# An attention, GLU and expert kernel: the loop for surplus tokens moves ahead of the last products, and a tile's state products move up behind its output products

## Chip, cores and metric

The kernel runs on one core of a Trainium2 chip. The metric is the device time in microseconds (us) of one execution. The version before the change takes 868.49 us, the median of three runs (866.66 to 868.85).

## What is computed

Three stages follow each other on 3072 tokens (4 sequences of 768) of width 384. Cut to what matters:

```python
# 1. gated linear attention, 8 heads of 48 per token
state = alpha_t[:, None] * state + outer(k_t, v_t)      # 48 x 48 per head
y_t = q_t @ state
# 2. rms norm, then a gated unit of width 1536
xn = x / sqrt(mean(x * x) + 1e-6) * rms_g
z = (silu(xn @ w_gate) * (xn @ w_val)) @ w_out
# 3. one of 8 experts per token
e = argmax(z @ r_gate)
out = prob(e) * sigmoid(z @ r_ogate)[e] * (relu(z @ w1[e]) @ w2[e])
```

## The kernel before

**Tiles of tokens.** The attention goes over 24 tiles of 128 tokens. Tiles 0 to 17 take the first three sequences in turn (tile t is block t // 3 of sequence t % 3), tiles 18 to 23 the fourth sequence. `stages(t)` (L410) yields five functions for a tile, in this order: `score` (L420, products at L425), `ktr` (L440, transposes of k at L445, copied to `kn` by ScalarE at L447), `outp` (L452, products of the output `ps_y` at L456 and L460), `state` (L474, products `ps_st` at L481, added to the state by VectorE at L488) and `xtr` (L492, transposes at L502). The products of L460 and L481 have the same form: a weight tile of 128 x 64, 48 columns. The last block of a sequence has no `state` (L475), and the first block of one has no L456.

**The order on TensorE.** The gated unit works on 8 groups of three tiles. For each it loops over 12 blocks of the hidden width, and each block has three slots: `m_gate` (L589, nine products `ps_g`), `m_val` (L608, nine products `ps_v`) and `m_out` (L630, nine products `ps_o` of the block before). Between slots the loop asks whether a stage of the attention is due (L861, L1087); if so, `stage()` (L850) takes the next function of `att_stream` (L844), so that one stage's products go between two slots. Five stages per tile are counted (`NST`, L796). From the group loop on, `seq` (L211) keeps the products in the order of the program; in the four runs before it (L868) the framework's scheduler may still shift them.

**The experts.** Tokens are scattered to a bucket per expert. The experts, sorted by their number of tokens, get fixed capacities (`SLOTS`, L92) and are worked off in nine parts by `e_h` (L1025, products `ps_h`, then ScalarE and VectorE write `h` at L1031 and L1032) and `e_o` (L1036, products `ps_b` at L1047). `e_fin` (L1052) scales a result on ScalarE (L1059) or VectorE (L1061) and sends it out by an indirect DMA that POOL issues (L1063). The products of the last part for the last four blocks are done after the loop over the parts (L1237 to L1240):

```python
    for i in range(parts[u][3]):
        for _, j in lag:
            e_o(u, j, [i])
        e_fin(u, i)
```

**The loop for surplus tokens.** Tokens beyond a capacity are handled by a loop over `nblk` blocks of 128 (L1251), behind all of this. `nblk` is computed on the chip (`beyond`, L1141) and read into a register of each engine (L1223). The loop's body has its own products, transfers and DMA issues on all five engines. In this execution it is passed by with no iteration: no instruction of lines 1252 to 1325 stands in the trace. L1353 is the kernel's end (drains and barriers), L1342 its start.

Of the kernel before, what the change touches and what calls it, by code (L numbers as in the profile page):

```python
# [8 lines left out]
F32 = mybir.dt.float32  # L9
F32R = mybir.dt.float32r  # L10
BF16 = mybir.dt.bfloat16
I32 = mybir.dt.int32
AF = mybir.ActivationFunctionType
ALU = mybir.AluOpType
AX = mybir.AxisListType
PSUM = bass.MemoryType.PSUM
DRAM = bass.MemoryType.DRAM
OFF = bass.IndirectOffsetOnAxis
# [25 lines left out]
    'LEADG': 6,  # L44
    'NAT': 5,
    'XO': 2,
    'STRICT': 4,
    'PET': 7,
    'NO': 'arkq',
# [5 lines left out]
def gla_glu_moe_kernel(  # L55
# [16 lines left out]
    nc = tc.nc  # L72
    P = 128
    B, H, S, D = q.shape
    NT, DM = out.shape
    NP = H // 2
    NCH = S // P
    NTILE = NT // P
    KD = DM // P
# [3 lines left out]
    E, _, F2 = w1.shape  # L83
    KF2 = F2 // P
    GT = 3
# [755 lines left out]
    spread[0] = False  # L841
    prep.extend(prework(GT))

    att_stream = (st for t in range(GT, NTILE) for st in stages(t))  # L844
    nprep = GT + 1
    AHEAD = CFG['AHEAD']
    done = 0
# [293 lines left out]
    def beyond():  # L1141
# [25 lines left out]
        nc.vector.memset(obk, 0.0)  # L1167
        return tot, cb, cbx, pid, obk

    lag = []  # L1170
    pw = []

    def load_next(p):
        for i in range(4):
            pw.append((load_w1, p, i))
            pw.append((load_w2, p, i))
# [24 lines left out]
    for u in range(U):  # L1201
        for j in range(KF2):
            if u == 0 and j < 2:
                continue
            if u == U - 1 and j > 3:
                pop_o()
            e_h(u, j)
            lag.append((u, j))
            if j == 0:
                if u > 1:  # L1210
                    pop_o()
                    pop_o()
            elif j > 1 and u < U - 1:
                pop_o()
            if u and j == 0 and u + 1 < U:
                load_rows(u + 1, ers[(u + 1) % 2])
            if u and u + 1 < U and j in TRJ:
                prep_rows(u + 1, TRJ.index(j))
            for _ in range(STEPS[u][j] if u < 2 else 1):
                weight_step()  # L1220
            if u == 2 and j == 1:
                tot, cb, cbx, pid, obk = beyond()
                nblk = nc.values_load(tot[0:1, 0:1], min_val=0, max_val=NM + E)  # L1223
        if u == 0:
            pop_o()
            prep_rows(1, 0)
            prep_rows(1, 1)
            prep_rows(1, 2)
            pop_o()
        if u >= 1 and u + 1 < U:  # L1230
            while ready or pw:
                weight_step()
            if parts[u + 1][0] + 1 < E:
                addresses(parts[u + 1][0] + 1)
                load_next(parts[u + 1][0] + 1)
    u = U - 1
    for i in range(parts[u][3]):  # L1237
        for _, j in lag:
            e_o(u, j, [i])
        e_fin(u, i)  # L1240

    psE.release()
    psM.release()
    xp.release()
    wpool.release()


    with ExitStack() as ov:
        op_ = ov.enter_context(tc.tile_pool(name="op", bufs=1, side="right", reuse_waits="tile"))
        pp = ov.enter_context(tc.tile_pool(name="pp", bufs=2, space=PSUM))  # L1250
        with tc.For_i(0, nblk, 1):  # L1251
            def sm(nm, w=1, dt=F32):
                return op_.tile([P, w], dt, tag=nm, name=nm)
            V = nc.vector
            ge = sm("ge", E)
            V.tensor_scalar(out=ge, in0=cb, scalar1=obk[:, 0:1], scalar2=None, op0=ALU.is_le)
            ef = sm("ef")
            V.tensor_reduce(out=ef, in_=ge, op=ALU.add, axis=AX.X)
            oh = sm("ohx", E)
            V.tensor_scalar(out=oh, in0=io8[:, 0, :], scalar1=ef[:, 0:1], scalar2=None, op0=ALU.is_equal)  # L1260
            V.tensor_tensor(out=ge, in0=oh, in1=cnt[:, 0, :], op=ALU.mult)
            ne = sm("ne")
            V.tensor_reduce(out=ne, in_=ge, op=ALU.add, axis=AX.X)
            V.tensor_tensor(out=ge, in0=oh, in1=cbx, op=ALU.mult)
            sl = sm("sl")
            V.tensor_reduce(out=sl, in_=ge, op=ALU.add, axis=AX.X)
            V.tensor_tensor(out=sl, in0=obk, in1=sl, op=ALU.subtract)
            V.tensor_tensor(out=ge, in0=oh, in1=capE[:, :, 0], op=ALU.mult)
            ce = sm("ce")
            V.tensor_reduce(out=ce, in_=ge, op=ALU.add, axis=AX.X)  # L1270
            V.scalar_tensor_tensor(out=sl, in0=sl, scalar=float(P), in1=ce, op0=ALU.mult, op1=ALU.add)
            V.tensor_tensor(out=sl, in0=sl, in1=pid[:, 0:1], op=ALU.add)
            rw = sm("rw")
            V.scalar_tensor_tensor(out=rw, in0=ef, scalar=float(REG), in1=sl, op0=ALU.mult, op1=ALU.add)
            ri = sm("ri", 1, I32)
            V.tensor_copy(ri, rw)
            V.tensor_tensor(out=sl, in0=sl, in1=ne, op=ALU.is_lt)
            V.scalar_tensor_tensor(out=rw, in0=sl, scalar=FAR, in1=rw, op0=ALU.mult, op1=ALU.add)
            zi = sm("zi", 1, I32)
            V.tensor_copy(zi, rw)  # L1280
            nc.gpsimd.indirect_dma_start(out=bucket[:, :], out_offset=OFF(ap=zi[:, 0:1], axis=0),
                                         in_=zrow[:, 0, :], in_offset=None,
                                         bounds_check=E * REG - 1, oob_is_err=False)
            r0 = nc.values_load(ri[0:1, 0:1], engines=[mybir.EngineType.SP], min_val=0, max_val=E * REG - P)
            wi = sm("wi", KD + KF2, I32)
            wf = sm("wf", KD + KF2)
            e3 = sm("e3", 2)
            V.tensor_scalar(out=e3[:, 0:1], in0=ef, scalar1=float(DM), scalar2=None, op0=ALU.mult)
            V.tensor_scalar(out=e3[:, 1:2], in0=ef, scalar1=float(F2), scalar2=None, op0=ALU.mult)
            V.tensor_scalar(out=wf[:, 0:KD], in0=pid[:, 1:1 + KD], scalar1=e3[:, 0:1], scalar2=None, op0=ALU.add)  # L1290
            V.tensor_scalar(out=wf[:, KD:], in0=pid[:, 1 + KD:], scalar1=e3[:, 1:2], scalar2=None, op0=ALU.add)
            V.tensor_copy(wi, wf)
            xr = sm("xr", RW)
            nc.sync.dma_start(xr[:, :], bucket[bass.ds(r0, P), :])
            wa = op_.tile([P, KD, F2], F32, tag="wa", name="wa")
            wb = op_.tile([P, KF2, DM], F32, tag="wb", name="wb")
            for i in range(KD):
                nc.gpsimd.indirect_dma_start(out=wa[:, i, :], out_offset=None,
                                             in_=w1.rearrange("e k n -> (e k) n"),
                                             in_offset=OFF(ap=wi[:, i:i + 1], axis=0))  # L1300
            for i in range(KF2):
                nc.gpsimd.indirect_dma_start(out=wb[:, i, :], out_offset=None,
                                             in_=w2.rearrange("e k n -> (e k) n"),
                                             in_offset=OFF(ap=wi[:, KD + i:KD + i + 1], axis=0))
            pt = pp.tile([P, KD, P], F32, tag="pt", name="ptx")
            for i in range(KD):
                nc.tensor.transpose(pt[:, i, :], xr[:, i * P:i * P + P], ident)
            xo = op_.tile([P, KD, P], F32, tag="xo", name="xo")
            V.tensor_copy(xo, pt)
            po = pp.tile([P, DM], F32, tag="po", name="po")  # L1310
            for j in range(KF2):
                ph = pp.tile([P, P], F32, tag="ph", name="ph")
                for i in range(KD):
                    nc.tensor.matmul(ph, lhsT=wa[:, i, j * P:j * P + P], rhs=xo[:, i, :],
                                     start=(i == 0), stop=(i == KD - 1))
                ht = op_.tile([P, P], F32, tag="ht", name="ht", bufs=2)
                nc.scalar.activation(ht, ph, AF.Relu)
                nc.tensor.matmul(po, lhsT=ht, rhs=wb[:, j, :], start=(j == 0), stop=(j == KF2 - 1))
            yo = sm("yo", DM)
            V.tensor_scalar(out=yo, in0=po, scalar1=xr[:, DM:DM + 1], scalar2=None, op0=ALU.mult)  # L1320
            ti = sm("ti", 1, I32)
            V.tensor_copy(ti, xr[:, RW - 1:RW])
            nc.gpsimd.indirect_dma_start(out=out[:, :], out_offset=OFF(ap=ti[:, 0:1], axis=0),
                                         in_=yo[:, :], in_offset=None, bounds_check=NT - 1, oob_is_err=False)
            V.tensor_scalar(out=obk, in0=obk, scalar1=1.0, scalar2=None, op0=ALU.add)
    act.release()


# [29 lines left out]
```

## Time and profile before

| | |
|---|---|
| runs, us | 868.85, 868.49, 866.66 |
| profiled execution, us | 865.15 |
| its span from first to last instruction, us | 863.4 |
| TensorE (PE) busy | 840.6 us, 97% |
| VectorE (DVE), ScalarE (ACT), POOL busy | 57%, 38%, 16% |
| granted TensorE clock, mean | 0.996 of full speed |

The profiled execution's own time is 1.75 us over its span, and 3.34 us under the median of the runs. A busy share says how long an engine had something in work; products are pipelined, so the start of one product to the start of the next is the better measure of TensorE's pace. "PEld" is TensorE's loading of weights. Names like POOLq stand for an engine's sequencer, which handles waits, branches and the issue of DMAs.

### The profile page before, as it was taken

To read this page: it belongs to the slowest core of one execution; us is meant where nothing else is said; L and a number is where in the kernel's file an instruction comes from. 1 tells how busy PE (TensorE), PEld (TensorE's weight loads), DVE (VectorE), ACT (ScalarE), POOL (GpSimd) and SP (SyncE) were. 2 spreads that over 40 slices of the span, in tenths; PEclk is the share of its full clock that TensorE was granted. 3 is DMA by queue.
4 is the path that set the end of the run, shared out by engine and by line. 5 is a ranking of instruction groups with operands and counts; after the bars stand their busy time and mean duration, and the time that the engine had idled before them with its cause. 6 is when DMAs were issued, how large, how long until landed. Compare 5 with 4: busy or idle time off the path is not lost.

```text
span 863.4 us, 15649 instructions
## 1 busy us (share of the span) xinstructions
PE 840.6 (97%) x6036; PEld 806.6 (93%) x6036; DVE 491.0 (57%) x1111; ACT 324.7 (38%) x705; POOL 142.2 (16%) x204
## 2 busy tenths in 40 slices
PE   7999999999999999999999999999999999999994
PEld 5899989999999999999999999999998999999994
DVE  7998988577765655765655632343534343444320
ACT  2655543333323332333433332333235343345431
POOL 2100000001100100100010010013124242434331
PEclk9999999999999999999999999999999999999998
DMA  9964555852322222222232000041065165256510
GB/s 192 205 164 147 177 128 140 213 138 80 97 60 54 63 49 60 75 74 52 52 88 60 10 29 1 2 130 63 16 203 196 37 210 169 72 165 202 185 39 24
DMA packets 120268, 88.96 MB, mean 103 GB/s; under 512 B 55291, under 2 KB 115324, under 8 KB 120192
## 3 DMA queue, kind: packets, MB, share of 16 engines
q1 hardware_dynamic: 115728, 78.46, 34.5%
q0 software_dynamic: 4464, 9.48, 3.1%
q8 instruction: 48, 0.79, 0.4%
q14 instruction: 28, 0.23, 0.1%
HBM read 72.11 MB, written 16.07 MB: 102 GB/s over the span
## 4 chain that ended last, share of the span: by engine, by line
PE 79%; DVE 7%; issue 5%; DMA 4%; POOL 2%; SPq 1%; ACT 1%; POOLq 0%; DVEq 0%; ACTq 0%
PE ps_o L638 17%; PE ps_v L604 16%; PE ps_g L604 16%; PE ps_b L1047 9%; PE ps_h L604 9%; PE ps_s L425 3%; DMA st<-in_moe_w_dram 3%; PE ps_y L460 2%; PE ps_y L456 2%; PE ps_st L481 1%; SPq L915 1%; PE ps_k L445 1%; PE ps_x L502 1%; PE ps_t L1011 1%; POOL out_dram L1063 1%
## 5 line engine op out<-in xcount | busy, mean ns | idle before, releaser
L615 DVE TENSOR_TENSOR tt<-tt,ps_v 128x384 f32<-128x384 f32 x96 | 52.9, 551 | 119.8 <-PE ps_v L604 116.8
L618 ACT ACTIVATE hh<-tt 128x384 fp32r<-128x384 f32 x96 | 50.3, 524 | 125.2 <-DVE tt L615 119.5
L596 ACT ACTIVATE tt<-ps_g 128x384 f32<-128x384 f32 x96 | 47.1, 490 | 130.4 <-PE ps_g L604 127.3
L624 DVE TENSOR_TENSOR hl<-tt,hh 128x384 fp32r<-128x384 f32 x96 | 54.4, 566 | 27.5 <-ACT hh L618 27.3
L1032 DVE SCALAR_TENSOR_TENSOR h<-ps_h,h 128x256 fp32r<-128x256 f32 (+6 forms) x72 | 38.0, 531 | 54.2 <-ACT h L1031 53.7
L1047 PE MATMUL ps_b<-w2a,h 128*128 128x384 f32 (+2 forms) x336 | 67.4, 339 | 1.5 <-ACT h L1031 1.5
L604 PE MATMUL ps_v<-xh,wvh 128*128 128x384 f32 x192 | 66.8, 348 | 1.9 <-DVE tt L615 1.9
L604 PE MATMUL ps_g<-xh,wgh 128*128 128x384 f32 x192 | 67.9, 353 | 0.1
L638 PE MATMUL ps_o<-woh,hh 128*128 128x400 f32 x192 | 66.6, 355 | 0.4 <-ACT hh L618 0.4
L638 PE MATMUL ps_o<-wol,hh 128*128 128x400 f32 x192 | 66.4, 346 | 0.0
L1047 PE MATMUL ps_b<-w2b,h 128*114 128x384 f32 (+3 forms) x336 | 65.0, 338 | 0.2 <-ACT h L1031 0.2
L604 PE MATMUL ps_g<-xl,wgh 128*128 128x384 f32 x192 | 64.9, 338 | 0.0
L604 PE MATMUL ps_v<-xh,wvl 128*128 128x384 f32 x192 | 64.9, 338 | 0.0
L604 PE MATMUL ps_g<-xh,wgl 128*128 128x384 f32 x192 | 64.8, 338 | 0.0
L604 PE MATMUL ps_v<-xl,wvh 128*128 128x384 f32 x192 | 64.6, 336 | 0.0
L638 PE MATMUL ps_o<-woh,hl 128*128 128x400 f32 x192 | 63.5, 344 | 0.0
L1047 PEld LDWEIGHTS ps_b<-w2a,h 128*128 128x128 f32 (+2 forms) x336 | 57.5, 181 | 2.7 <-ACT h L1031 2.2
L1047 PEld LDWEIGHTS ps_b<-w2b,h 128*114 128x114 f32 (+3 forms) x336 | 57.5, 175 | 2.1 <-ACT h L1031 0.6
L604 PE MATMUL ps_h<-x,w1b 128*128 128x456 f32 (+3 forms) x288 | 58.4, 343 | 0.0
L1031 ACT ACTIVATE h<-ps_h 128x256 fp32r<-128x256 f32 (+6 forms) x72 | 33.4, 468 | 63.3 <-PE ps_h L604 63.1
L604 PE MATMUL ps_h<-x,w1a 128*128 128x256 f32 (+3 forms) x288 | 53.4, 327 | 0.0
L467 POOL TENSOR_SCALAR ss<-ss 128x1 f32<-128x1 f32 x24 | 5.9, 245 | 282.1 <-ACT xn L466 279.3
(284 smaller groups left out, 1966.0 us busy)
## 6 DMA issues: line engine op xcount, KB each, us to landing
st<-in_moe_w_dram SPq DMA_DIRECT2D x64, 384.0 KB, 4.6
bucket<-zero SPq DMA_DIRECT2D x8, 772.0 KB, 6.2
stg<-in_moe_w_gate_dram SPq DMA_DIRECT2D x12, 384.0 KB, 4.1
stg<-in_moe_w_val_dram SPq DMA_DIRECT2D x12, 384.0 KB, 4.2
stg<-in_moe_w_out_dram SPq DMA_DIRECT2D x12, 384.0 KB, 3.7
v<-in_v_dram SPq DMA_DIRECT2D x23, 192.0 KB, 3.0
blk_a<-in_alpha_dram SPq DMA_DIRECT2D x34, 96.0 KB, 2.4
blk_k<-in_k_dram SPq DMA_DIRECT2D x34, 96.0 KB, 2.2
```

The costliest lines, as they stand in the source:

```text
L425: seq(nc.tensor.matmul(ps[hh][:, p, :], lhsT=kT[r, p, :], rhs=qT[r, p, :], start=True, stop=True))
L456: seq(nc.tensor.matmul(ps[:, p * 2 * D:p * 2 * D + 2 * D], lhsT=qT[:, p, :], rhs=S_[:, p, :], start=(p == 0), stop=False, skip_group_check ...
L460: seq(nc.tensor.matmul(ps[u, h * D:h * D + D], lhsT=Pt[h % 2][:, h // 2, u], rhs=vt[t][:, h, :], start=first, stop=True, skip_group_check= ...
L596: nc.scalar.activation(tt, ps, AF.Silu)
L604: seq(nc.tensor.matmul(ps, lhsT=a_[:, kc, :], rhs=b_[:, kc, :], start=(n == 0), stop=(n == 3 * KD - 1)))
L615: nc.vector.tensor_tensor(out=tt, in0=tt, in1=ps, op=ALU.mult)
L618: nc.scalar.activation(hh, tt, AF.Copy)
L624: nc.vector.tensor_tensor(out=hl, in0=tt, in1=f(hh), op=ALU.subtract)
L638: seq(nc.tensor.matmul(obank[s][i], lhsT=a_[:, sl], rhs=weight(b_, j), start=(j == j0 and n == 0), stop=(j == j1 - 1 and n == 2)))
L1031: nc.scalar.activation(hh[:, 0, :], ps, AF.Relu)
L1032: nc.vector.scalar_tensor_tensor(out=hh[:, 1, :], in0=ps, scalar=0.0, in1=f(hh[:, 0, :]), op0=ALU.max, op1=ALU.subtract)
L1047: ins = nc.tensor.matmul(ob2[u][i][0:r], lhsT=hh[:, a_, sl], rhs=we[p][b_][:, j, :], start=(j == 0 and m == 0), stop=(j == KF2 - 1 and m = ...
```

## The change

A new generator `four(t)` stands for `stages(t)` from tile 6 on (`MT`). It still gives five functions per tile: score, transposes of k, then output products with the state products right behind them, then a function that does nothing, then the transposes of x. What the engines do with the two results after the products is called in the order output, state.

The loop for surplus tokens is now in a function `overflow()`, called behind the loop over the parts and ahead of the last 36 products and their three transfers. It stands in a condition of its own, `tc.If(nblk > 0)`. Its banks for results come from the pool of the experts, and its tiles take the place of the pool `xp`. The body is the same otherwise.

```diff
+    'MT': 6,
...
-    att_stream = (st for t in range(GT, NTILE) for st in stages(t))
+    def four(t):
+
+        s_, k_, y_, d_, x_ = stages(t)
+
+        def yd_():
+            posts = [y_(), d_()]
+
+            def post():
+                for p in posts:
+                    if p:
+                        p()
+            return post
+
+        def no_():
+            return None
+        return s_, k_, yd_, no_, x_
+
+    att_stream = (st for t in range(GT, NTILE) for st in (four if t >= CFG['MT'] else stages)(t))
...
+    def overflow():
+        xp.release()
+        op_ = tc.alloc_tile_pool(name="op", bufs=1, side="right", reuse_waits="tile")
+        with tc.If(nblk > 0):
+            with tc.For_i(0, nblk, 1):
...
+        return op_
...
+    op_ = overflow()
     u = U - 1
     for i in range(parts[u][3]):
         for _, j in lag:
             e_o(u, j, [i])
         e_fin(u, i)
 
+    op_.release()
     psE.release()
     psM.release()
-    xp.release()
     wpool.release()
-
-
-    with ExitStack() as ov:
-        op_ = ov.enter_context(tc.tile_pool(name="op", bufs=1, side="right", reuse_waits="tile"))
-        pp = ov.enter_context(tc.tile_pool(name="pp", bufs=2, space=PSUM))
-        with tc.For_i(0, nblk, 1):
...
```

## Rows read from the trace of the kernel before

**Rows 1.** Busy time by stretch: us, then busy us (instructions) of each engine, clock.

```profile
140.00:200.00 60.00, 60.00 (x491) 57.35 (x490) 39.21 (x91) 20.79 (x50) 2.61 (x8) 1.00 0.60 152
200.00:330.00 130.00, 130.00 (x1044) 124.65 (x1043) 85.05 (x204) 44.29 (x105) 14.42 (x28) 1.00 0.29 74
330.00:545.00 215.00, 215.00 (x1634) 207.45 (x1633) 117.77 (x276) 72.91 (x173) 16.43 (x33) 1.00 0.18 46
```

**Rows 2.** Timeline of PE: start, length; state products between ps_g and ps_v.

```profile
302.35 0.34 PE L604 MATMUL ps_g<-xh,wgl 128*128 128x384 f32 x1
...
302.62 0.67 PE L481 MATMUL ps_st<-v,kn 128*64 128x48 f32 x16
...
303.50 0.34 PE L604 MATMUL ps_v<-xl,wvh 128*128 128x384 f32 x1
```

**Rows 3.** Timeline of PE: output products between ps_v and ps_o.

```profile
321.12 0.34 PE L604 MATMUL ps_v<-xh,wvle 128*128 128x384 f32 x1
321.29 1.03 PE L456 MATMUL ps_y<-wide,qT 128*128 128x96 f32 x8
322.25 1.14 PE L460 MATMUL ps_y<-v,P 128*64 128x48 f32 x32
...
323.60 0.34 PE L638 MATMUL ps_o<-wol,hh 128*128 128x400 f32 x1
```

**Rows 4.** Timeline of PE at tile 6: output and state products together.

```profile
139.03 0.42 PE L604 MATMUL ps_g<-xh,wgle 128*128 128x384 f32 x1
...
141.22 0.64 PE L481 MATMUL ps_st<-v,kn 128*64 128x48 f32 x16
...
142.06 0.34 PE L604 MATMUL ps_g<-xl,wghe 128*128 128x384 f32 x1
```

**Rows 5.** Line L481 from 150 to 520 us: count, ns min/median/max.

```profile
L481 PE MATMUL ps_st<-v,kn x208: 222/222/257, 163.7 to 516.2; 128*64 128x48 f32 x104
```

**Rows 6.** Timeline of ACT: the copy of kn in the tile of rows 3.

```profile
316.72 0.60 ACT L447 ACTIVATE kn<-ps_k 128x512 f32<-128x512 f32 x1 [1.51 <-PE ps_k L445]
```

**Rows 7.** Timeline of all engines near the end.

```profile
833.15 1.64 POOL L1063 DMA_INDIRECT out_dram<-ob,ix  x1 [0.31 <-issue]
...
842.15 2.94 PE L604 MATMUL ps_h<-x,w1b 128*128 128x336 f32 x18
...
844.93 6.46 PE L1047 MATMUL ps_b<-w2b,h 128*112 128x384 f32 x36
...
845.62 0.51 DVE L1032 SCALAR_TENSOR_TENSOR h<-ps_h,h 128x336 fp32r<-128x336 f32 x1 [0.88 <-ACT h L1031]
...
852.29 0.93 POOL L1063 DMA_INDIRECT out_dram<-ob,ix  x1 [1.10 <-ACT ob L1059]
```

**Rows 8.** Line L1251, the loop's own instructions: count, ns min/median/max, first and last start.

```profile
L1251 POOLq EVENT_SEMAPHORE  x16: 17/43/2288, 853.1 to 858.0; - x16
...
L1251 PEldq EVENT_SEMAPHORE  x13: 51/51/51, 851.4 to 858.1; - x13
...
L1251 PEldq COMPARE_BRANCH  x3: 97/179/325, 848.8 to 858.2; - x3
...
L1251 POOLq INC_SWDGE_SEM  x1: 1224/1224/1224, 855.6 to 855.6; - x1
```

**Rows 9.** Line L1353, the kernel's end: the same columns.

```profile
L1353 POOLq DRAIN  x3: 40/103/4327, 858.3 to 863.2; - x3
```

**Rows 10.** Line L1342, the kernel's start: the same columns.

```profile
L1342 POOLq DRAIN  x1: 174/174/174, 0.4 to 0.4; - x1
```

**Rows 11.** Line L1223, reading nblk into registers: the same columns.

```profile
L1223 DVEq TENSOR_LOAD <-tab x1: 824/824/824, 849.4 to 849.4; - x1
```

**Rows 12.** Waits of POOL in 840 to 864 us: total, times, longest.

```profile
POOL out_dram L1063 <- ACT ob L1059: 14.4, 2, 13.3
```

**Rows 13.** Line L1063: the time from issue to landing.

```profile
DMA to landing us min/median/max: 2.7/6.1/9.4
```

**Rows 14.** The page's DMA queues: packets, MB, share of 16 engines' span.

```profile
q8 instruction: 48, 0.79, 0.4%
```

More of the change, by code (lines that the diff above doesn't have):

```diff
@@ L1168, in beyond, with sm @@
         return tot, cb, cbx, pid, obk
+    def overflow():
[3 more added lines that the diff above has]
+            with tc.For_i(0, nblk, 1):
+                def sm(nm, w=1, dt=F32):
+                    return op_.tile([P, w], dt, tag=nm, name=nm)
+                V = nc.vector
+                ge = sm("ge", E)
+                V.tensor_scalar(out=ge, in0=cb, scalar1=obk[:, 0:1], scalar2=None, op0=ALU.is_le)
+                ef = sm("ef")
+                V.tensor_reduce(out=ef, in_=ge, op=ALU.add, axis=AX.X)
+                oh = sm("ohx", E)
+                V.tensor_scalar(out=oh, in0=io8[:, 0, :], scalar1=ef[:, 0:1], scalar2=None, op0=ALU.is_equal)
+                V.tensor_tensor(out=ge, in0=oh, in1=cnt[:, 0, :], op=ALU.mult)
+                ne = sm("ne")
+                V.tensor_reduce(out=ne, in_=ge, op=ALU.add, axis=AX.X)
+                V.tensor_tensor(out=ge, in0=oh, in1=cbx, op=ALU.mult)
+                sl = sm("sl")
+                V.tensor_reduce(out=sl, in_=ge, op=ALU.add, axis=AX.X)
+                V.tensor_tensor(out=sl, in0=obk, in1=sl, op=ALU.subtract)
+                V.tensor_tensor(out=ge, in0=oh, in1=capE[:, :, 0], op=ALU.mult)
+                ce = sm("ce")
+                V.tensor_reduce(out=ce, in_=ge, op=ALU.add, axis=AX.X)
+                V.scalar_tensor_tensor(out=sl, in0=sl, scalar=float(P), in1=ce, op0=ALU.mult, op1=ALU.add)
+                V.tensor_tensor(out=sl, in0=sl, in1=pid[:, 0:1], op=ALU.add)
+                rw = sm("rw")
+                V.scalar_tensor_tensor(out=rw, in0=ef, scalar=float(REG), in1=sl, op0=ALU.mult, op1=ALU.add)
+                ri = sm("ri", 1, I32)
+                V.tensor_copy(ri, rw)
+                V.tensor_tensor(out=sl, in0=sl, in1=ne, op=ALU.is_lt)
+                V.scalar_tensor_tensor(out=rw, in0=sl, scalar=FAR, in1=rw, op0=ALU.mult, op1=ALU.add)
+                zi = sm("zi", 1, I32)
+                V.tensor_copy(zi, rw)
+                nc.gpsimd.indirect_dma_start(out=bucket[:, :], out_offset=OFF(ap=zi[:, 0:1], axis=0),
+                                             in_=zrow[:, 0, :], in_offset=None,
+                                             bounds_check=E * REG - 1, oob_is_err=False)
+                r0 = nc.values_load(ri[0:1, 0:1], engines=[mybir.EngineType.SP], min_val=0, max_val=E * REG - P)
+                wi = sm("wi", KD + KF2, I32)
+                wf = sm("wf", KD + KF2)
+                e3 = sm("e3", 2)
+                V.tensor_scalar(out=e3[:, 0:1], in0=ef, scalar1=float(DM), scalar2=None, op0=ALU.mult)
+                V.tensor_scalar(out=e3[:, 1:2], in0=ef, scalar1=float(F2), scalar2=None, op0=ALU.mult)
+                V.tensor_scalar(out=wf[:, 0:KD], in0=pid[:, 1:1 + KD], scalar1=e3[:, 0:1], scalar2=None, op0=ALU.add)
+                V.tensor_scalar(out=wf[:, KD:], in0=pid[:, 1 + KD:], scalar1=e3[:, 1:2], scalar2=None, op0=ALU.add)
+                V.tensor_copy(wi, wf)
+                xr = sm("xr", RW)
+                nc.sync.dma_start(xr[:, :], bucket[bass.ds(r0, P), :])
+                wa = op_.tile([P, KD, F2], F32, tag="wa", name="wa")
+                wb = op_.tile([P, KF2, DM], F32, tag="wb", name="wb")
+                for i in range(KD):
+                    nc.gpsimd.indirect_dma_start(out=wa[:, i, :], out_offset=None,
+                                                 in_=w1.rearrange("e k n -> (e k) n"),
+                                                 in_offset=OFF(ap=wi[:, i:i + 1], axis=0))
+                for i in range(KF2):
+                    nc.gpsimd.indirect_dma_start(out=wb[:, i, :], out_offset=None,
+                                                 in_=w2.rearrange("e k n -> (e k) n"),
+                                                 in_offset=OFF(ap=wi[:, KD + i:KD + i + 1], axis=0))
+                pt = psE.tile([P, KD, P], F32, tag="h", name="ptx", bufs=2)
+                for i in range(KD):
+                    nc.tensor.transpose(pt[:, i, :], xr[:, i * P:i * P + P], ident)
+                xo = op_.tile([P, KD, P], F32, tag="xo", name="xo")
+                V.tensor_copy(xo, pt)
+                po = psE.tile([P, DM], F32, tag="tr", name="po", bufs=1)
+                for j in range(KF2):
+                    ph = psE.tile([P, P], F32, tag="h", name="ph", bufs=2)
+                    for i in range(KD):
+                        nc.tensor.matmul(ph, lhsT=wa[:, i, j * P:j * P + P], rhs=xo[:, i, :],
+                                         start=(i == 0), stop=(i == KD - 1))
+                    ht = op_.tile([P, P], F32, tag="ht", name="ht", bufs=2)
+                    nc.scalar.activation(ht, ph, AF.Relu)
+                    nc.tensor.matmul(po, lhsT=ht, rhs=wb[:, j, :], start=(j == 0), stop=(j == KF2 - 1))
+                yo = sm("yo", DM)
+                V.tensor_scalar(out=yo, in0=po, scalar1=xr[:, DM:DM + 1], scalar2=None, op0=ALU.mult)
+                ti = sm("ti", 1, I32)
+                V.tensor_copy(ti, xr[:, RW - 1:RW])
+                nc.gpsimd.indirect_dma_start(out=out[:, :], out_offset=OFF(ap=ti[:, 0:1], axis=0),
+                                             in_=yo[:, :], in_offset=None, bounds_check=NT - 1, oob_is_err=False)
+                V.tensor_scalar(out=obk, in0=obk, scalar1=1.0, scalar2=None, op0=ALU.add)
+        return op_
@@ L1240, in gla_glu_moe_kernel @@
         e_fin(u, i)
+    op_.release()
     psE.release()
     psM.release()
-    xp.release()
     wpool.release()
-    with ExitStack() as ov:
-        op_ = ov.enter_context(tc.tile_pool(name="op", bufs=1, side="right", reuse_waits="tile"))
-        pp = ov.enter_context(tc.tile_pool(name="pp", bufs=2, space=PSUM))
-        with tc.For_i(0, nblk, 1):
[L1252 to L1325, printed above, removed]
```

## The prediction

> **What bounds the kernel now.** I read the share of each engine by stretch first. From 140 to 545 us TensorE has work in flight in all of the time, while VectorE works 39 of 60, 85 of 130 and 118 of 215 us [rows 1]: in the stretch where tiles 7 to 23 pass, the end moves with what TensorE is given, and with nothing else. Then I read the timeline of TensorE around single stages, start against start, since a busy engine may still lose time between products. Last I read the end: the last product ends at 844.93 + 6.46 = 851.39 us, and the span at 863.4, so 12.0 us have no product; a list of line L1251 and L1353 says what is in them.
>
> A difference under 0.3%, 2.6 us, can't be told from no change here.
>
> **State products behind the output products.** Inside a slot products start every 0.175 us (the 36 of ps_b: 6.46 less one length of 0.34, over 35 [rows 7]; 321.12 to 321.29 in [rows 3]). State products alone: from the last ps_g at 302.35 to the second ps_v at 303.50 are 1.15 us, where two steps would be 0.35, so the stage costs 0.80 us [rows 2]. Output products alone: 321.12 to 323.60 is 2.48, less 0.35, so 2.13 us [rows 3]. Tile 6 happens to show both together before the change: 139.03 to 142.06 is 3.03, less 0.35, so 2.68 us [rows 4]. The state products thus cost 0.55 us in company against 0.80 alone. Of the 0.55, 0.09 belong to the place, since that stage began 0.26 after the product before it and the one of rows 3 began 0.17 after. The other way of counting: 16 starts, spaced as the 32 of the same form in rows 3 (1.14 less one length of 0.22 [rows 5], over 31: 0.030 us), make 0.47. I take a saving of 0.80 - 0.48 = 0.32 us; the bounds are 0.25 and 0.33.
>
> From 150 to 520 us line L481 has 208 products, 16 per tile: 13 tiles, 7 to 14 and 18 to 22 [rows 5]; tile 6 has nothing left to win, and the others have no state products. One of the 13 shares its place with products of the routing already and I give it 0.2. The sum is 12 x 0.32 + 0.2 = 4.0 us, between 3.2 and 4.3.
>
> What could eat it: the state products read kn, which ScalarE writes from 316.72 to 317.32, in a tile whose output products begin at 321.29 [rows 6, 3]; 4 us of cover, so no wait. Without that cover each tile would lose what is missing. The result's bank is freed by the masks that the output products wait for anyway. The add of the state (L488) stands on VectorE behind ScalarE's square of the output, and it waits some 0.5 us for products already under way; behind it on VectorE stands the gated unit's product for ps_v, which is later on TensorE too. The slot that loses its stage gives VectorE and ScalarE 0.80 us less, but 21 of a group's 36 slots have no stage at all (15 stages in three tiles), and rows 1 show no wait there. No DMA is moved by this part: the load of v stays in the fifth stage. SP's and POOL's queues keep their order.
>
> **The loop leaves the end.** Behind the last DMA issue, which lasts from 852.29 to 853.22 [rows 7], POOL waits 2.29 us for the landing, until 855.4, spends 1.22 on INC_SWDGE_SEM from 855.6, then works off some 12 waits until its drain begins at 858.3 [rows 8, 9]. That drain takes 4.33 us, and the end comes 0.8 behind it. With the loop gone from here, POOL is free for its drain at 853.2, 1.8 us behind the last product, beside the landing. The trace has no drain under these circumstances. Nearest in place is the one of 4.33; the shortest, at the start of the kernel, takes 0.17 [rows 10]. With 4.33 the end comes 1.8 + 4.33 + 0.8 = 6.95 us behind the last product instead of 12.0, 5.05 less. With 0.17 the landing sets the end: 4.0 + 0.2 + 0.8 = 5.0, so 7.0 less. If the drain begins only behind the landing, 4.0 + 4.33 + 0.8 = 9.15, so 2.85 less. I take 5.05, because the 4.33 stands in the same place and nothing in the new place holds POOL back; the ends of the range are 2.85 and 7.0, and zero if the drain waits for something that I don't see.
>
> **The loop enters the middle.** It now stands between the last ps_h, which end at 842.15 + 2.94 = 845.09, and the first of the 36 ps_b, which started at 844.93 [rows 7]. TensorE has to read nblk, branch, wait for its own last product, branch again. Reading and first branch cost nothing: the sequencer did its first branch at 848.8 with products running until 851.39 [rows 8, 7], and this lead of 2.6 us covers them. The rest is exposed: 0.16 of overlap lost, 0.05 for the wait, 0.33 for the longest branch, some 0.2 for a weight load, and 0.15 of gaps. I estimate 0.9 us. It can't be under 0.3 (overlap, wait and the shortest branch of 0.10); above, it is 3.7 if all engines wait for each other as they do now behind the loop. That is worked out so: VectorE's last piece of h ends at 846.13 [rows 7], its read of nblk takes 0.82 [rows 11], two branches 0.1, the 12 waits 1.4 (from 856.9 to 858.3) and TensorE's branch 0.33, so 848.8.
>
> POOL's share is hidden. Its last issue ends at 834.8 [rows 7] and it then waits 13.3 us for ScalarE [rows 12]. The landing takes 9.4 at most [rows 13], from 833.15 to 842.6; 1.22 and even a drain of 4.33 behind that end at 848.1, where the next issue came before and now comes 0.9 later. With less cover, the three transfers at the end would begin later by what is missing. SP has nothing left to do. The reads of nblk by ScalarE and VectorE move ahead of the last three results, which aren't due before 847 (12 products behind 844.93). The indirect DMAs of the loop don't run.
>
> **The sum**, against the profiled execution's own 865.15 us: -4.0 - 5.05 + 0.9 = -8.15, so 857.0. The median is 3.34 above this execution, and I forecast the same difference there: 868.49 - 8.15 = 860.3 us.
>
> **Rivals.** *The drain is short.* Its 4.33 may be the tail of INC_SWDGE_SEM, the one thing that POOL did behind its issues; at the kernel's start, with no transfer yet, both are short. Then 858.4. *The drain follows the landing*: 862.5. *The jump costs a code fetch.* Code comes in by a queue of its own, 48 packets in 0.4% of 16 engines' span, 1.15 us each [rows 14]; today no stretch of TensorE's work contains a jump, so the trace neither shows nor excludes a stall. If the code behind the loop's body has to be fetched first, add 1.2 to 2: 861.9.
> The Trainium skill, Runtime: NRT & Kernel Launch, section Instruction fetch mechanics, says that a taken branch whose target lies outside the two blocks held by an engine forces such a fetch before it goes on. By that rule this rival holds if the body reaches over the window; no row here shows it.
> *The state products gain nothing*, because what follows a stage waits or is shifted by the scheduler where order is not kept (tiles 7 and 8); against it speak tile 6 and rows 1: 864.3. *The engines meet at the condition, without a drain*: 3.7 instead of 0.9, 863.1. *Slower than before:* the condition is a full meeting of the engines with POOL's drain inside: 848.5 when all have arrived and waited (as above), 4.33 of drain, 0.8 to the release: 853.6, a hole of 8.5 us in TensorE, while the end keeps a drain behind the landing. -4.0 + 8.5 - 2.85 = +1.65: 870.1. This decides from a hole of 6.85 us on. For it: today's skipped loop does end in such a meeting. Against it: the meeting belongs to the loop's exit, and the condition passes by the loop with its exit.
>
> **Chances and range.** Forecast 0.33 (its own range 858.8 to 861.6); short drain 0.24; drain behind the landing 0.12; code fetch 0.11; state products without gain 0.06; meeting without drain 0.05; slower 0.05; 0.04 for another order by the scheduler, of either sign. The range 856.5 to 865.0 runs from the short drain with the upper bound of the first part and a run's scatter (868.85 to 866.66) to the state products without gain. Faster by over 0.3% (under 865.9): 0.87; the slower rival at its price and the edges of two others are within 0.3%: 0.10; slower 0.03.
>
> **What would show it.** Line L481 without a group of its own from 150 us on; output and state products together near 2.6 us; TensorE still without a wait there. A pause of TensorE of some 0.7 us between the last ps_h and the first ps_b at L1047, and INC_SWDGE_SEM well ahead of the last issues. From the last product to the end 7 us, with the length and the start of POOL's last drain. A hole over 3 us at the condition, or 10 us and more behind the last product, would make the forecast wrong.

## The result, and the profile after

The changed kernel takes 857.19 us, the median of four runs (855.82 to 857.58), beside 867.58 us for the kernel before (865.88 to 868.85). The ratio is 0.9872, with a 95% interval of 0.9845 to 0.99. The profiled execution takes 857.01 us with a span of 855.2 us at a mean granted clock of 0.998. A second timing on another chip gave 858.14 beside 867.99 us, 0.9881 (0.9851 to 0.9912). The forecast was 860.3 us, a ratio of 0.9906: inside the second interval, just over the edge of the first, and 3.1 us above the time, which lies outside the forecast's own range of 858.8 to 861.6 and inside the whole one. The profiled execution fell by 8.14 us, from 865.15 to 857.01, where the sum forecast 8.15. That agreement is partly luck, as a division of the span shows. The borders are starts of single products in the timeline of TensorE (products of ps_g are counted from 0).

| stretch, us | before | after | difference | forecast |
|---|---|---|---|---|
| start to ps_g no. 108 | 120.56 | 120.26 | -0.30 | 0 |
| ps_g no. 108 to no. 720: 13 joined tiles | 410.30 | 406.04 | -4.26 | -4.0 |
| on to the first ps_h | 80.57 | 80.40 | -0.17 | 0 |
| first ps_h to last ps_h: experts | 233.35 | 234.53 | +1.18 | 0 |
| last ps_h to the end of the last product | 6.61 | 6.98 | +0.37 | +0.9 |
| last product to the end of the span | 12.04 | 6.99 | -5.05 | -5.05 |

The second stretch begins and ends with these two products before the change:

```profile
120.56 0.42 PE L604 MATMUL ps_g<-xh,wgh 128*128 128x384 f32 x1
...
530.86 0.34 PE L604 MATMUL ps_g<-xh,wghe 128*128 128x384 f32 x1
```

and with these after it:

```profile
120.26 0.42 PE L605 MATMUL ps_g<-xh,wgh 128*128 128x384 f32 x1
...
526.30 0.34 PE L605 MATMUL ps_g<-xh,wghe 128*128 128x384 f32 x1
```

The three touched stretches give 8.94 us. The expert stage gave 1.2 back, and it is the stretch that scatters: in the eleven other profiles below it takes 232.9 to 235.3 us, 235.27 in a second profile of the kernel before itself.

**The joined tile.** TensorE's timeline after the change, at the tile of [rows 3]: start, length, engine, line, operation.

```profile
318.60 0.34 PE L605 MATMUL ps_v<-xh,wvle 128*128 128x384 f32 x1
318.78 1.03 PE L457 MATMUL ps_y<-wide,qT 128*128 128x96 f32 x8
319.73 1.14 PE L461 MATMUL ps_y<-v,P 128*64 128x48 f32 x32
320.70 0.64 PE L482 MATMUL ps_st<-v,kn 128*64 128x48 f32 x16
321.27 0.45 PE L639 MATMUL ps_o<-woh,hh 128*128 128x400 f32 x1
321.56 0.34 PE L639 MATMUL ps_o<-wol,hh 128*128 128x400 f32 x1
```

From the last ps_v to the second ps_o are 321.56 - 318.60 = 2.96 us; less two steps of 0.175 that is 2.61. Apart, the two groups cost 2.13 and 0.80 by the same count [rows 2, 3], so 0.32 us is saved at this place. The state products begin 0.97 behind the start of the group before them, with no gap of their own, and the wide products behind them start late (0.57, then 0.29) as they do behind any such group.

**The condition.** Timeline near the end, all engines; the number in brackets is the engine's idle time before the row, and what ended it.

```profile
840.67 0.51 DVE L1050 SCALAR_TENSOR_TENSOR h<-ps_h,h 128x336 fp32r<-128x336 f32 x1 [1.57 <-ACT h L1049]
841.38 2.09 PE L1065 MATMUL ps_b<-w2b,h 128*112 128x384 f32 x11
842.06 0.51 DVE L1050 SCALAR_TENSOR_TENSOR h<-ps_h,h 128x336 fp32r<-128x336 f32 x1 [0.89 <-ACT h L1049]
843.59 4.29 PEld L1065 LDWEIGHTS ps_b<-w2b,h 128*112 128x112 f32 x25 [0.45 <-issue]
843.62 4.59 PE L1065 MATMUL ps_b<-w2b,h 128*112 128x384 f32 x25
844.92 0.95 POOL L1081 DMA_INDIRECT out_dram<-ob,ix  x1 [13.68 <-ACT ob L1077]
...
848.25 0.58 ACT L1077 ACTIVATE ob<-ps_b,er 112x384 f32<-112x384 f32 x1 [3.61 <-PE ps_b L1065]
849.11 0.93 POOL L1081 DMA_INDIRECT out_dram<-ob,ix  x1 [1.11 <-ACT ob L1077]
```

The scheduler put 11 of the last 36 products ahead of the condition, against the order of the program. The pause stands behind them: weights are not loaded for 0.45 us. From the first to the last start of the 36 are 843.62 + 4.59 - 0.34 - 841.38 = 6.49 us, where [rows 7] give 6.12, so the condition costs TensorE 0.37. The condition's own instructions on the sequencers (count, ns min/median/max, first and last start):

```profile
L1192 POOLq COMPARE_BRANCH  x1: 45/45/45, 827.4 to 827.4; - x1
L1192 POOLq INC_SWDGE_SEM  x1: 1164/1164/1164, 839.2 to 839.2; - x1
...
L1192 PEldq COMPARE_BRANCH  x1: 367/367/367, 842.7 to 842.7; - x1
...
L1192 PEldq EVENT_SEMAPHORE  x1: 51/51/51, 843.5 to 843.5; - x1
```

TensorE has one branch and one wait now; before it had three branches and 13 waits [rows 8]. The branch, 0.37 us from 842.7, ends at about 843.0, while products run until 841.38 + 2.09 = 843.47: hidden. POOL's INC_SWDGE_SEM ends at 840.4, 4.5 us ahead of its next issue: hidden too.

**The end.** The kernel's end, line L1374, the same columns:

```profile
L1374 SPq EVENT_SEMAPHORE  x14: 17/28/11398, 840.4 to 855.1; - x14
...
L1374 POOLq DRAIN  x3: 40/112/5501, 848.9 to 854.9; - x3
```

POOL's drain is on its queue from 848.9, ahead of the last issue's own 0.93 us, and ends 5.50 later at 854.4. The issue ends at 849.11 + 0.93 = 850.04, so 4.33 us of drain lie behind it, the same 4.33 as in [rows 9]. SP's wait for the last landing, 11.4 us from 840.4, is over at 851.8: the landing is hidden behind the drain. From the last product, which ends at 843.62 + 4.59 = 848.21, to 855.2 are 6.99 us.

### The profile page after: what moved, and what is told of

Its sections match the earlier page's. It is cut to its first block, busy times and chain, and to the rows that moved or that the text cites. A ratio compares the mean times of both kernels' runs of the same rounds, so it can differ in the third digit from the quotient of the medians.

```text
span 855.2 us, 15586 instructions
## 1 busy us (share of the span) xinstructions
PE 837.4 (98%) x6036; PEld 805.9 (94%) x6036; DVE 495.6 (58%) x1111; ACT 323.7 (38%) x705; POOL 146.3 (17%) x204
## 4 chain that ended last, share of the span: by engine, by line
PE 77%; DVE 7%; DMA 7%; issue 4%; POOL 1%; ACT 1%; SPq 1%; POOLq 0%; DVEq 0%; ACTq 0%
PE ps_o L639 17%; PE ps_g L605 16%; PE ps_v L605 16%; PE ps_b L1065 8%; PE ps_h L605 8%; DMA st<-in_moe_w_dram 4%; PE ps_s L426 3%; PE ps_y L461 2%; PE ps_y L457 2%; DMA out_dram<-ob,ix 1%; DMA er<-bucket 1%; PE ps_st L482 1%; PE ps_k L446 1%; PE ps_x L503 1%; DMA blk_q<-in_q_dram 1%
## 5 line engine op out<-in xcount | busy, mean ns | idle before, releaser
L468 POOL TENSOR_SCALAR ss<-ss 128x1 f32<-128x1 f32 x24 | 8.3, 345 | 273.8 <-ACT xn L467 271.1
```

## Experiments

**Each part alone.** The first kernel joins the state products and keeps the loop at the end; the second moves the loop and joins nothing.

The first, against the change (the loop's line stands where it stood before):

```diff
-    op_ = overflow()
...
+        with tc.For_i(0, nblk, 1):
```

The second, against the change:

```diff
-    'MT': 6,
+    'MT': 99,
```

> The state products join the output products from tile 6 on; the loop for surplus tokens stays at the end. If the two parts add up, the first expert product comes 4.5 to 4.8 us earlier than before (13 tiles at 0.34), some of it is given back in the first experts (0 to 1.2 us), and the last 12.0 us behind the last product stay as they were: 3.4 to 4.8 us less than before. If the gain of the change came from the end alone, no difference.

> The loop moves ahead of the last products under its condition; the state products stay in a slot of their own. If the parts add up: 0.4 us lost in the pause at the condition, 5.0 us won behind the last product, so 4.6 us less than before. If the expert stage gives back what the gated stage wins only because TensorE arrives earlier, no give-back shows here; if the give-back of about 1.2 us comes from the loop's move, it shows here.

Measured: 0.9961 (0.9943 to 0.998) for the join, 864.72 beside 867.31 us, and 0.9948 (0.9925 to 0.9971) for the loop, 862.42 us. The product of the two is 0.9909, -7.9 us. The borders of the gated stage, ps_g no. 108 and no. 720, in the kernel with the join alone:

```profile
120.92 0.42 PE L605 MATMUL ps_g<-xh,wgh 128*128 128x384 f32 x1
...
526.96 0.34 PE L605 MATMUL ps_g<-xh,wghe 128*128 128x384 f32 x1
```

and in the kernel with the loop moved alone:

```profile
120.39 0.42 PE L605 MATMUL ps_g<-xh,wgh 128*128 128x384 f32 x1
...
530.68 0.34 PE L605 MATMUL ps_g<-xh,wghe 128*128 128x384 f32 x1
```

That is 406.04 against 410.29 us; before it is 410.30. The whole gain of the join lies in this stage. Followed from product to product, the ps_g of the changed kernel fall back by 0.47 us against those of before where the state products now stand, and gain 0.81 where they stood: 0.34 net in each of the last ten tiles, and 0.34, 0.29 and 0.22 in the first three. The tail is 12.07 us in the first kernel and 7.00 in the second, the pause 0 and 0.39. So the parts don't act on each other in these stretches, and the rival in which the state products gain nothing falls. The loop's move gave what was expected (4.9 us between the medians, 4.6 expected). The join gave less: 2.6 us between the medians, 3.4 by the ratio, where 3.4 to 4.8 were expected. The expert stage takes 234.90 and 234.58 us in these two profiles, 1.55 and 1.23 more than in the first profile of the kernel before, so its give-back shows with either part alone.

**Is it the interruption, or the change of form?** A saving per stage could also be a fixed price for breaking into the wide products. Here the output products stand alone as before, and `dx_` calls the state products and then the transposes of x, which have another form (128 x 128).

```diff
-        return s_, k_, yd_, no_, x_
+        return s_, k_, y_, no_, dx_
```

> The change, but the state products are joined with the transposes of x (right ahead of them) instead of the output products. Theory: the 0.34 us per tile come from a change of form (weight tiles of 128 x 64 beside 128 x 128) that the joined products save; then little is won here, under 0.1 us per tile, and the whole is 3 to 4.5 us slower than the change. Rival: each interruption of the gated unit's products costs a fixed 0.34 us; then this kernel is as fast as the change, within 0.5 us.

Measured: 862.62 us, 0.994 (0.9917 to 0.9964), what the loop alone gives; the gated stage takes 410.86 us. Timeline of TensorE at one such pair:

```profile
330.76 0.35 PE L639 MATMUL ps_o<-wohe,hl 128*128 128x400 f32 x1
331.04 0.67 PE L482 MATMUL ps_st<-v,kn 128*64 128x48 f32 x16
331.64 0.55 PE L503 MATMUL ps_x<-ident,xn 128*128 128x128 f32 x3
331.94 0.42 PE L605 MATMUL ps_g<-xh,wghe 128*128 128x384 f32 x1
332.20 0.34 PE L605 MATMUL ps_g<-xl,wghe 128*128 128x384 f32 x1
```

and the transposes alone, in the changed kernel:

```profile
327.59 0.34 PE L639 MATMUL ps_o<-wohe,hl 128*128 128x400 f32 x1
327.77 0.49 PE L503 MATMUL ps_x<-ident,xn 128*128 128x128 f32 x3
328.02 0.42 PE L605 MATMUL ps_g<-xh,wghe 128*128 128x384 f32 x1
328.28 0.34 PE L605 MATMUL ps_g<-xl,wghe 128*128 128x384 f32 x1
```

Counted as above, the pair costs 332.20 - 330.76 - 0.35 = 1.09 us and the transposes alone 0.34; with 0.80 for state products alone, joining saves 0.05 where it saved 0.32 beside the output products. (The stage is 0.6 longer than before, not 0.6 shorter, since TensorE once waits 0.6 us for VectorE, ahead of the transposes of k; ps_g starts fall back by about 0.9 between no. 216 and no. 252 and gain some 0.06 per tile from there on.) So the price is not that of an interruption as such. The rows fit a price for the change of form. The state products start 0.28 us behind the wide product before them (0.27 in [rows 2]), while the transposes alone, whose weight tile is 128 x 128 like that of the wide products, start after a plain step of 0.18; the second wide product comes late behind either (0.26 to 0.28). The reverse order, transposes first, was not run.

**Does the condition make the engines meet?** The loop stays at the end, within the condition and with nothing joined.

```diff
+        with tc.If(nblk > 0):
             with tc.For_i(0, nblk, 1):
```

> The kernel before with the condition nblk > 0 put around the loop, which stays at the end; the state products stay in a slot of their own. If the engines' meeting (12 waits each) belongs to the loop's exit, the condition takes it away: 1.4 us less, the end 10.6 us behind the last product (landing 4.0, INC_SWDGE_SEM 1.2, drain 4.3, barrier 0.8, gaps). If the condition ends in such a meeting itself, 12.0 us as before.

Measured: 866.3 us, 0.9982 (0.9956 to 1.0008), no change that can be told; but the tail is 10.81 us against 12.04. The condition's instructions there:

```profile
L1251 POOLq EVENT_SEMAPHORE  x4: 17/43/2429, 854.6 to 857.2; - x4
...
L1251 PEldq EVENT_SEMAPHORE  x1: 51/51/51, 853.0 to 853.0; - x1
...
L1251 POOLq INC_SWDGE_SEM  x1: 1224/1224/1224, 857.3 to 857.3; - x1
```

and the kernel's end behind them:

```profile
L1354 POOLq DRAIN  x3: 40/107/4324, 858.6 to 863.5; - x3
```

The 16 waits of POOL and 13 of TensorE in [rows 8] are 4 and 1, though the loop is still in the program: the meeting belongs to the loop's exit, and the condition passes it by. POOL's wait for the landing (2.43 us), its 1.22 and its 4.32 of drain stay in line, as long as the condition stands behind the last issue.

The other way round, the loop stands in the middle without its condition; the rest is the change.

```diff
-        with tc.If(nblk > 0):
-            with tc.For_i(0, nblk, 1):
+        with tc.For_i(0, nblk, 1):
```

> The change with the bare loop in its new place, without the condition around it. If the meeting of the engines belongs to the loop's exit, TensorE waits in the middle until all engines have arrived: by my sum 3.7 us instead of the change's 0.4, so about 3.3 us slower than the change; if POOL's landing and INC_SWDGE_SEM are late there as well, up to 5 us slower. If moving alone did it, as fast as the change.

Measured: 862.34 us, 0.9939 (0.9915 to 0.9963). TensorE's pause and its sequencer's work in it, first the timeline:

```profile
848.04 2.09 PE L1065 MATMUL ps_b<-w2b,h 128*112 128x384 f32 x11
...
848.72 0.51 DVE L1050 SCALAR_TENSOR_TENSOR h<-ps_h,h 128x336 fp32r<-128x336 f32 x1 [0.88 <-ACT h L1049]
...
852.28 4.64 PE L1065 MATMUL ps_b<-w2b,h 128*112 128x384 f32 x25 [2.15 <-issue]
```

then the loop's line:

```profile
L1192 PEldq EVENT_SEMAPHORE  x13: 51/51/51, 850.2 to 851.9; - x13
...
L1192 PEldq COMPARE_BRANCH  x3: 101/187/325, 849.4 to 852.0; - x3
```

The 36 products take 852.28 + 4.64 - 0.34 - 848.04 = 8.54 us from first to last start, so the pause is 2.42, and the meeting's share of it 2.42 - 0.37 = 2.05 us. The prediction had 3.7 for this pause. Its chain fits: from VectorE's last h (848.72 + 0.51 = 849.23) to the next product 3.05 us pass, where the forecast had 848.8 - 846.13 = 2.7. The pause is smaller because the 11 products put ahead of the loop fill 2.1 us of it, and so the kernel loses 2.05 us against the change at this place, not the 3.3 expected. The tail is 7.07.

**Is the drain the tail of INC_SWDGE_SEM?** No loop at all: this kernel leaves out the handling of surplus tokens, and so the condition, the branches and INC_SWDGE_SEM.

```diff
-        with tc.If(nblk > 0):
...
```

> The change without the loop for surplus tokens, which handles none in these inputs; it leaves that handling out. No condition, no pause, no INC_SWDGE_SEM. If POOL's last drain has its 4.3 us from INC_SWDGE_SEM, the drain is short here and the end comes 5.0 us behind the last product instead of 7.0; together with the pause of 0.4 us that is 2.4 us less than the change. If the drain takes 4.3 us behind any last DMA that POOL issued, the end stays 7.0 us behind the last product and only the pause goes: 0.4 us less than the change.

Measured: 860.92 us, 0.9906 (0.9875 to 0.9936). The last issue, in the timeline:

```profile
853.71 0.93 POOL L1081 DMA_INDIRECT out_dram<-ob,ix  x1 [1.10 <-ACT ob L1077]
```

and the drain, at the kernel's end:

```profile
L1298 POOLq DRAIN  x3: 40/174/5497, 853.5 to 859.9; - x3
```

The issue ends at 854.64 and the drain at 853.5 + 5.5 = 859.0: 4.33 behind, with no INC_SWDGE_SEM in the program. The rival of a short drain falls. The pause is gone too (6.12 from first to last start), so 0.37 is what the condition costs. This kernel is no faster than the change all the same. Its tail is 7.35, since 1.19 us pass from the drain's end to the end of the span where the change has 0.82; that takes back the 0.37, and why it is longer isn't shown. Its profiled execution had a low clock at the start (last section), and only two of its seven runs had a mean granted clock of 0.998; these took 857.04 and 857.05 us, as long as the change (855.82 to 857.58 in its first timing).

**Does the end follow the last issue?** The copy of the last result is split between ScalarE and VectorE, to issue earlier.

```diff
+        if u == U - 1 and i == parts[u][3] - 1:
+            H = DM // 2
+            nc.scalar.activation(ob[:, 0:H], ob2[u][i][0:r, 0:H], AF.Copy, scale=er[0:r, i, DM:DM + 1])
+            nc.vector.tensor_scalar(out=ob[:, H:], in0=ob2[u][i][0:r, H:], scalar1=er[0:r, i, DM:DM + 1],
+                                    scalar2=None, op0=ALU.mult)
+        elif i % 2 == 0:
-        if i % 2 == 0:
```

> The change, with the copy of the very last result split between ScalarE (columns 0 to 191) and VectorE (192 to 383). If POOL's drain ends 4.33 us behind the end of POOL's last issue, an earlier issue moves the end by the same amount: the copy took 0.58 us whole, a half some 0.35 to 0.4, so 0.2 us from the tail of 6.99, to 6.8, and nothing elsewhere; the time 0.2 us under the change's, too little to tell in the medians. If the drain hangs on something else (the landing of earlier transfers), the tail stays at 7.0. If one engine's half waits behind the other's read of the same bank, the tail is 7.2 or more.

Measured: 860.74 us, 0.9918 (0.9889 to 0.9948): no gain. The timeline shows that the halves ran one behind the other:

```profile
848.53 0.42 ACT L1078 ACTIVATE ob<-ps_b,er 112x192 f32<-112x192 f32 x1 [3.61 <-PE ps_b L1065]
848.98 0.42 DVE L1079 TENSOR_SCALAR ob<-ps_b,er 112x192 f32<-112x192 f32 x1 [1.93 <-ACT ob L1078]
849.68 0.94 POOL L1086 DMA_INDIRECT out_dram<-ob,ix  x1 [1.40 <-DVE ob L1079]
```

VectorE waits for ScalarE, and the two together take 0.87 us instead of 0.58. The issue comes 0.3 us later, ending at 850.62; the drain ends at 854.95, again 4.33 behind, and the tail is 7.30 instead of 6.99. As an attempt it failed; as a test it shows the end moving with POOL's last issue, by the same amount.

**More tiles joined.** All tiles from the fourth on, timed twice, the second time beside the unaltered change and on the same chip.

```diff
-    'MT': 6,
+    'MT': 3,
```

> As the change, but the state products join from tile 3 on. If each tile is worth 0.34 us where TensorE is the bound, up to 1.0 us less than the change; TensorE had idle time in that stretch (60 to 140 us: 77.9 of 80 us with work), so between 0 and 1.0 us, and a loss of up to 1 us if the scheduler shifts the order there.

> The whole change, unaltered, timed in more rounds. If its two parts simply add, the ratio is the product of the two measured alone, 0.9961 x 0.9948 = 0.991, some 859.5 us beside 867.3. If they help each other (or the four runs of the first comparison are the true figure) it is 0.987, some 856.3 us. By stage either theory expects the same profile: from ps_g no. 108 to no. 720 406.0 us, a pause of 0.4 us at the condition, 7.0 us from the last product to the end; what is left must lie in the expert stage (233.2 to 235.3 us in the profiles so far).

> State products joined from the fourth tile on (MT = 3) in place of the seventh, beside the unaltered change on the same chip. If a joined tile always gives 0.3 us, three more tiles give 0.9 us and the ratio is 0.001 under that of the change; if tiles 3 to 5 gain nothing, as their stage showed in the first profile (ps_g no. 108 at the same time), the two ratios agree within 0.001. A gap of 0.0017, as the two first comparisons had, would speak for a gain outside that stage.

Measured first: 856.19 us, 0.9855 (0.9828 to 0.9881). In that profile ps_g no. 108 came at 121.13, as in the change, and I read this as no gain from tiles 3 to 5. Then, side by side: 853.4 us, 0.9842 (0.9813 to 0.9871), for MT = 3 and 858.14 us, 0.9881, for the change. The expectation that the two agree within 0.001 fell, and so did my reading. Busy time by stretch (columns as in [rows 1]) of the first MT = 3 kernel:

```profile
15.00:30.00 15.00, 15.00 (x144) 12.05 (x143) 11.90 (x26) 7.12 (x20) 1.86 (x4) 0.67 1.19 204
```

and of the second:

```profile
15.00:30.00 15.00, 14.26 (x202) 11.43 (x200) 14.79 (x36) 8.58 (x25) 2.65 (x6) 1.00 1.20 200
```

The first profile had a mean granted clock of 0.67 in this stretch, and TensorE did 144 products instead of 202. Its first ps_g started at 37.60, not 34.39. So like has to be compared with like. At a clock of 1.00 ps_g no. 108 starts at 118.21 with MT = 3 and at 120.26 in the change (-2.05); at 0.67 and 0.66, at 121.13 and 123.48 in the re-timed change (-2.35). At 1.00, two other kernels with MT = 6, the join alone and the split copy, have 120.92 and 120.85 there. Of the 2.05, 0.95 are won by ps_g no. 90, as three joined tiles would give by the price above (1.0), and 1.10 from there to no. 108. The waits of TensorE from 34 to 121 us in the change name that second part:

```profile
PE ps_v L605 <- DVE tt L616: 1.6, 1, 1.6
```

In the MT = 3 kernel this wait isn't there, in either profile (ps_g no. 90 to no. 108 takes 11.94 us instead of 13.04); why the join removes it isn't shown. From ps_g no. 108 to no. 720 the two kernels take 406.04 and 405.99. The medians differ by 4.7 us, more than these 2; the expert stage of the profile is 1.6 shorter, which I can't tell from its scatter. MT = 3 is the best version found, by 2 us that the trace places and by more in the timing, where the two intervals still overlap.

**The kernel before once more**, a single execution, to place its first profile:

> The kernel before once more, for a second trace of it. If the 1.2 us that the change gave back in the first experts (TensorE's pauses at 626 to 645 us) are scatter of the transfers, the starts of the expert products between 625 and 685 us differ between the two traces of this kernel by as much; if they belong to the change, the two traces agree within 0.2 us.

Measured: 867.82 us, span 866.1, with 410.30 us in the gated stage and 12.11 at the end, as in the first profile. The 2.7 us more are 0.35 ahead of ps_g no. 108, 0.35 from no. 720 to the first ps_h, and 1.92 in the expert stage (235.27 against 233.35). The waits of TensorE in it:

```profile
PE ps_t L1011 <- DMA er<-bucket: 1.8, 2, 1.0
PE ps_b L1047 <- ACT h L1031: 1.4, 4, 0.7
PE ps_b L1047 <- issue: 0.2, 1, 0.2
```

The first profile has 1.1 us for the tokens from the bucket, so when these transfers land differs between two executions of one program; that is 0.7 of the 1.92, and these rows don't name the rest. Between 625 and 685 us the starts of the expert products fall back by 0.95 us from the first to the second profile of this kernel, where the change fell back by 1.14: most of the give-back is scatter, as the first alternative had it.

## Why the prediction was right and where it was wrong

**State products, -4.0: right in kind, measured -4.26.** The term mis-sized is "a saving of 0.80 - 0.48 = 0.32 us": the two costs are 0.81 and 0.47, so 0.34 in most tiles, the 0.47 being what the other way of counting, by the spacing of the same form, had given. Ten tiles at 0.34 and 0.85 for the first three make 4.25; one of these, with 0.22, is as poor as the one that I gave 0.2. No wait of TensorE came up in that stage; the cover of 4 us for kn held.

**The end, -5.05: right, to 0.1 us.** The drain kept its 4.33 and began where POOL came free, beside the landing. Both rivals about it, short drain and drain behind the landing, are out by three kernels with the same distance: the change, no loop, the split copy.

**The pause, +0.9: right in kind, wrong in size, measured 0.37.** The failed term is the exposed sum of "0.16 of overlap lost, 0.05 for the wait, 0.33 for the longest branch, some 0.2 for a weight load, and 0.15 of gaps". I assumed a second branch behind the wait; there is only one, and it hides under the products ahead. Nor did the condition stand between the last ps_h and the first ps_b: 11 products had been put ahead of it. The lower bound of 0.3 held. The three touched terms add up to -8.94 instead of -8.15.

**From the profile to the median: wrong.** "The median is 3.34 above this execution, and I forecast the same difference there" is the step that failed most. The profiled execution fell by 8.14 us as the sum had it, and the offset shrank from 3.34 to 0.18; that is the whole miss of 3.1 us. The profiled execution before was a quick one: 865.15 us, with medians of 867.3 to 868.0 in the later timings and 867.82 for the second profile. The profiled execution after was an ordinary one, 0.18 under its median. The offset belonged to that execution and not to the kernel: of the 2.7 us by which the second profile is longer, 1.9 lie in the expert stage. That the profile agreed with the sum is luck: the three terms gave 0.8 us more than forecast and two untouched stretches 0.5, and the expert stage took 1.2 back. Taking 8.94 from 867.58 gives 858.6, a ratio of 0.9897, inside both intervals. What the medians fell beyond that, 1.5 us in the first timing and 0.9 in the second, is within their intervals of some 5 us; the clock at the start (last section), which differs from run to run, can make as much, and how much of it does I can't say. The number alone would have misled: 857.19 is nearer to the 858.4 of the short drain than to the forecast, and the drain kept its 4.33. By its own terms (858.4 less 0.3 and a scatter of 2.2) the low end of the range would lie near 856, not at 856.5; that decides nothing here.

**The other rivals.** The engines don't meet at the condition; at a bare loop they do, for 2.05 us more than the condition. The slower case needed a meeting and a drain there; neither took place. A code fetch at the jump did not show: the pause of 0.37 has no room for 1.2 to 2 us.
The Trainium skill, Runtime: NRT & Kernel Launch, section Instruction fetch mechanics, holds that a jump beyond the blocks at hand stalls for a fetch. No row here shows whether this jump reached that far, so the pause of 0.37 us neither bears the rule out nor speaks against it.

## What to carry to other kernels

Put narrow products of one form next to each other: the price is paid at the entry into the form and out of it, so joining equal forms saves it (0.32 us here) and joining unequal ones hardly does (0.05). Move what is rarely needed off the kernel's end to a place where every engine still has work, and guard the loop by a condition, since it is the loop's exit at which the engines meet. What the new place costs when the loop has work isn't shown, since it had none in these inputs. Take a forecast from the stage that moves, and treat the distance of one profile from the median as chance until a second profile shows the same.

## What the runs showed of the hardware

POOL's last drain takes 4.32 to 4.33 us in all 13 profiles, counted from where POOL comes free: right behind its last issue in the change (4.33), and 5.1 us behind it in the kernel before (issue until 853.2, drain from 858.3 [rows 7, 9]), when the landing had been over since 855.4. At the kernel's start a drain takes 0.17 [rows 10]. It is thus no wait for the landing, but what it does in that time is not shown.

In the middle a condition costs TensorE 0.37 us and a skipped loop 2.4; at the kernel's end the loop's exit costs 1.2 us more than a condition.

TensorE's clock falls in some executions right at the start, in four of the 13 profiles. From 15 to 30 us the re-timed change had a mean granted clock of 0.66 (0.50, the lower level of 1.2 GHz, from 15.5 to 25 us, and 1.00 from 26 us on):

```profile
15.00:30.00 15.00, 15.00 (x142) 11.62 (x141) 11.82 (x26) 7.07 (x20) 1.86 (x4) 0.66 1.20 201
```

The first profile of the change has 1.00:

```profile
15.00:30.00 15.00, 14.29 (x205) 11.45 (x203) 14.79 (x35) 8.70 (x25) 2.75 (x6) 1.00 1.16 203
```

The waits of TensorE from 5 to 15 us tell the two apart. The re-timed change has this one, near 10 us, and the first profile of the change has not:

```profile
PE ps_n L280 <- DMA nat<-in_k_dram: 0.3, 1, 0.3
```

A wait for this transfer, of 0.26 to 0.62 us, stands in the four profiles whose clock fell and in none of the nine others. Whether it brings the fall on isn't shown; the cause stays open. The first ps_g starts at 37.67 instead of 34.27, 3.4 us later. The profiles of the kernels without the loop, without the condition, and with MT = 3 the first time have the same start; their terms above are taken from later stages for that reason. The first two also had a clock of 0.50 from about 121 to 124 us, behind a wait of TensorE of 1.8 and 2.3 us for VectorE (a wait of 1.9 in the kernel before had no fall behind it), and their ps_g no. 108 starts at 125.5 and 125.9. It seems to reach the medians too, though these executions are not traced: of 57 timed executions of the kernel before that stood beside the experiments, 14 had a mean granted clock of 0.985 to 0.990 and a median of 870.85 us, the other 43 one of 0.992 to 0.996 and 866.94 us. A comparison of few runs depends on how many of each it drew; the four of the change in the first timing all had 0.998 or 0.999.
